# Clustered attention and a SoLU layer on one core: the first token block's turn moves to TensorE, the last block is scaled into w_in's place, and every engine's list is written anew

## The chip, the cores and the metric

The kernel runs on one core of one Trainium2 chip. The metric is the device time of one execution in microseconds (us), lower is better. Times before the change: 224.88 us, the median of three runs (224.47 to 226.29).

## The reference

Two parts follow each other. The first is attention in which a query sees only the keys of its own cluster; the second is a feed-forward layer over the heads' outputs.

```python
B, H, S, D = 4, 8, 768, 64                 # 16 clusters per head
q_assign = argmax(q_n @ c_n.T)             # q_n, k_n, c_n: rows divided by their norm
k_assign = argmax(k_n @ c_n.T)
mask = q_assign[..., :, None] == k_assign[..., None, :]
scores = where(mask, (q @ k.T) / sqrt(D), -1e9)
attn = exp(scores - max(scores)); attn = attn / sum(attn)
x = (attn @ v), as 3072 tokens x 512       # 4 x 768 tokens, 8 heads x 64
h = x @ w_in                               # 512 x 1024
sm = exp(h - max(h)) / sum(exp(h - max(h)))
solu = h * sm
ln = (solu - mean(solu)) / sqrt(var(solu) + 1e-6) * g_ln
out = ln @ w_out                           # 1024 x 512
```

## The kernel before

Everything is written as named operations that are added to a planner (class `Weave`). An operation has an engine, a cost, the operations that it needs, and a function that records its instructions. The order of the operations on each engine is not computed: it is written out by hand as five strings, `ORDER["PE"]` and so on, in which `S3` means the next three operations of kind S. A second table, `AWAY`, names operations that run on another engine than their default (ACT, DVE or POOL; the table "POOL" holds placements that would otherwise be DMAs of SP). The planner's costs do not set the order on an engine; the engines run their lists in order and wait on semaphores.

The names that the text uses, with the lines at which the profile shows them:

- **tp**, **xa**, **xb** (batch 0 only): PE turns 128 tokens of q or k into head-dim-first form (L395, L402), and a copy brings it from PSUM to SBUF (L421, L429). The later batches are turned by DVE, **xt** (L443).
- **ca**: cast of a turned q or k tile into the bf16 tile `qk` (L467 on ACT, L469 and L471 on DVE or POOL).
- **cl, tb, mx, oh, ot, pl, bl**: the clusters. PE's product with the centroids (L483, L488), then four DVE steps that find the best cluster and write it as one-hot (turn back L496, maximum L509, one-hot L514, turn L520), then the placement of the one-hot into `qk` as extra contraction rows (L532, L539) and a blank (L548). The scores then have the cluster match in them, so that exp gives 0 outside of the cluster.
- **S**: scores of one PSUM bank, two 256-column matmuls in most units (L626). **E**: exp of that bank on ACT (L634). **V**: six 65-column matmuls for attn @ v of 128 queries and one head (L653), the 65th column being the sum. **N**: DVE divides by it and writes the bf16 tile `x` (L665, L678). A V of a new group waits for the N of the group before, because there is one `ops` tile. S has three PSUM banks of its own, and the two first banks of `hreg` up to the feed-forward part.
- **cv**: cast of v to bf16 (L557). **su, ce**: g_ln is folded into w_out and its column mean taken off (L597, L606, DVE). **wi**: cast of w_in to bf16 into the tile `w_in_sb` (L577, POOL).
- For each of the 24 blocks f of 128 tokens: **tx** brings x into transposed form `xT` (L708, a DMA transpose issued by SP; block 23 by PE, L717, and a DVE copy, L720). **h**: x @ w_in in four pieces of two 512-column matmuls (L739), which fill two of the three banks of `hreg`. **hm**: the maximum (L745, DVE), **ex**: exp with its sum (L751, ACT), **u**: h times exp (L758, DVE), which frees the banks for later h. **bn, ag, at, al**: variance and the scale alpha (L769, L773 on DVE, L779 to L788 on POOL). **tu**: u transposed (L763 by DMA; blocks 22 and 23 by PE, L727, and a copy, L733 or L735). **y**: the product with w_out in four pieces (L808). **sc**: y times alpha (L826 on ACT, L828 on DVE). **ou**: the output DMA (L837); block 23 is written in two halves of 320 and 192 columns, the second (**oz**) by ACT's DMA queue.
- **wm** and **fl**: PE filler (L855), 25 and 2 matmuls each, that keep PE busy before there is work.

In the code before, `turned(f)` pairs the blocks of the first three batches, so that one DMA transpose of 256 rows brings blocks 0 and 1; `f_scale` puts the first half of block 23 into the tile `y`, which has two buffers, so that it waits for the output DMA of block 21.

Of the kernel before, what the change touches and what calls it, by code (L numbers as in the profile page):

```python
# [22 lines left out]
class Weave:  # L23
# [6 lines left out]
        ld4 si ld3 lv ld lg ld2 lo3 lv ld4 lv ld6 lo ld6 lv li4 tx ld3 tx lv2 ld2 tu ld3 lv ld2 tx  # L30
        tu ou ld6 tu ld5 lv tu ld6 ou ld7 tu ld lv ld4 lv ld3 tx ou lv ld2 tu ld2 ou tx ld4 ou tu
        ld3 tx ou ld4 tu ld7 lv2 ld4 tu lv ld6 ou tu2 pl2 ou tx ld6 tx ou lv tu pl3 tx ou2 tu2 lv tu
        pl tu tx ou tx ou tu tx ou tu tx ou2 tu tx ou tu2 ou tu ou6
    """
    ORDER["POOL"] = """
        pl2 bl pl2 ca bl pl cv pl z ca4 pl2 ca pl2 z bl ca cv2 sg pl4 bl ca pl2 z cv2 pl2 bl ca2 cv2
        ca wi8 ca pl4 ca z cv2 z ca2 at2 bl al ca2 pl3 cv ca pl at ca cv2 pl2 at al pl2 ca al cv2 bl
        at ca2 pl4 al ca bl ca3 pl ca cv pl5 ca al ca2 cv ca2 at2 cv pl2 al ca2 at pl3 ca cv at cv
        al pl bl cv ca3 al at pl2 ca pl2 bl al pl cv pl cv4 at bl ca3 at al2 pl ca al ca2 pl ca pl2
        ca at cv ca3 cv bl pl at pl3 bl al at cv2 po at2 al2 at2 al2 at2 al4 at2 al2 at al  # L40
    """
    ORDER["PE"] = """
        wm fl2 tp2 cp fl2 cl tp2 fl6 cl tp2 S3 cq tp S tp S2 tp2 S3 cl V2 S V S tp S tp S tp gt V3
        S2 tp3 S3 cl S2 V2 S2 V S6 V3 S3 cl S3 V4 S6 V2 S V2 S4 V2 S V2 S2 cl S2 V S V2 S V S2 me2
        S3 V4 S5 cl V S V3 S5 V2 S h4 S2 V2 h2 S3 V3 S V S h S h S2 h V S2 V3 S2 h S V2 S y4 S2 h S
        V S h S2 V3 S2 cl h2 S2 V4 S3 h2 S2 V2 S y2 S2 y S y h V S2 V2 S V S h2 S2 V h V S2 y4 S2 V2
        S cl S3 V4 S2 y S y S2 V2 S V S y S V S V2 S2 y S h S2 V4 S3 cl S V2 S2 cl S3 V2 h S V S V S
        h S2 h V S2 V2 S y S V S y3 V S2 V2 S V S h S h S2 h2 S2 V5 S3 h2 V y2 S3 y2 S2 h S V3 S2 h
        V h S V2 S cl h S3 V2 cl S2 h2 S2 V2 S y S h V2 S3 y3 V2 S h3 S V S2 V2 S V S y2 S2 y2 h V
        S2 V h V S V S2 V2 cl S2 h2 S3 cl S2 V2 S h S V4 S2 y3 S2 y V S2 h S V3 S2 h2 S3 cl V4 S3 y3  # L50
        V2 S y S2 h V2 h S2 h2 S h S h S V2 S y2 S V2 y S3 y V2 S2 h2 S V2 S y S h y3 S V S2 h2 S2 h
        V2 cl S V h2 S y S V S2 V2 S h S V2 S h S2 y V S2 y h2 V2 S2 V2 y S V2 S2 h S h S2 V S V h
        S2 V2 y2 h V S3 h2 S2 V3 S y S y h2 S2 V3 h2 S3 V y4 S h2 S2 V3 S h2 S3 V y2 h2 y2 S3 h2 S2
        V4 y S2 y3 h4 V2 y V2 y3 h ptx h y h2 y3 h2 y4 h2 ptu2 y9 ptu y3 ptu y4
    """
    ORDER["DVE"] = """
        cn xa cb ca2 tb mx oh ot pl2 tb mx xa oh ot xa cf xa3 cv ca tb mx ca oh ot ca gk su xa N xa
        su2 tb mx oh ot N su2 tb mx oh ot N xt N xt su N su xt su N tb xt mx ce N oh ce3 N ce4 hm ot
        N u tb mx N bn hm N bn oh ag ot u xt2 sc hm N bl tb u mx bn2 ca hm N oh ag ot bn u xt2 bn ag
        hm N sc u xt tb mx N oh cv ot bn3 ag xt N sc ca xt2 tb mx N bn oh ot ag tb N mx ca hm ca oh  # L60
# [1256 lines left out]
```

## Time and profile before

| | |
|---|---|
| median of the three runs | 224.88 us |
| the profiled execution, its time | 224.34 us |
| its span, first to last instruction | 222.5 us |
| PE busy | 216.2 us (97%) |
| DVE busy | 201.0 us (90%) |
| ACT busy | 192.9 us (87%) |
| POOL busy | 126.1 us (57%) |

Busy time of PE is the union of its matmuls with their modelled ends, so the time between two starts says more about PE than the busy share. The profile was taken in one execution of 224.34 us, 1.84 us more than the span; the median of the runs lies 0.54 us above that execution.

### The profile page before, as it was taken

How to read it: one execution, taken by the hardware profiler on the slowest of the kernel's cores; microseconds unless marked ns; L12 is line 12 of the kernel's file. 1: busy time of each engine (PE TensorE's matmuls, PEld its weight loads, DVE VectorE, ACT ScalarE, POOL GpSimd, SP SyncE). 2: the span in 40 equal slices, each digit the busy share in tenths (PEclk: the TensorE clock that was granted, in tenths of full speed). 3: DMA queues.
4: the chain of work that ended last, by engine and by line, in shares of the span. 5: the costliest groups of instructions: out<-in, count | busy, mean ns of one | idle time of the engine just before them, and what ended most of it. 6: DMA issues, size and time to landing. Idle time of an engine off the chain costs nothing.

```text
span 222.5 us, 6879 instructions
## 1 busy us (share of the span) xinstructions
PE 216.2 (97%) x2544; PEld 151.3 (68%) x2544; DVE 201.0 (90%) x364; ACT 192.9 (87%) x376; POOL 126.1 (57%) x255
## 2 busy tenths in 40 slices
PE   8999989999999999999999999999999999999993
PEld 7766667667677686877677767677677776665442
DVE  3899989999999999999999998999899698898892
ACT  2899999989999999999988999989899998793351
POOL 3189898937956847668538756628927121024051
PEclk9999999999999999999999999999999999999999
DMA  6999899999998988979998999897961229476533
GB/s 145 363 396 175 176 201 340 202 204 186 206 172 156 199 143 175 206 161 195 189 181 134 239 197 149 120 203 143 222 111 33 52 76 139 115 152 149 153 120 120
DMA packets 123025, 38.92 MB, mean 175 GB/s; under 512 B 111976, under 2 KB 117744, under 8 KB 122992
## 3 DMA queue, kind: packets, MB, share of 16 engines
q1 hardware_dynamic: 122272, 38.00, 82.6%
q10 hardware_dynamic: 720, 0.49, 0.7%
q8 instruction: 20, 0.33, 0.7%
q14 instruction: 13, 0.11, 0.2%
HBM read 23.11 MB, written 6.29 MB: 132 GB/s over the span
## 4 chain that ended last, share of the span: by engine, by line
PE 75%; DVE 16%; DMA 4%; issue 2%; POOL 1%; SPq 1%; DVEq 0%
PE sps L626 22%; PE yps L808 17%; PE hreg L739 17%; PE ops L653 12%; PE csc L488 4%; DVE w_out_c L606 2%; DMA out_dram<-y 2%; PE idle_p L855 2%; DVE w_sum L597 2%; DMA raw<-in_k_dram 2%; DVE oh L514 2%; DVE xt L429 1%; POOL qk L532 1%; DVE xt L443 1%; DVE nmax L745 1%
## 5 line engine op out<-in xcount | busy, mean ns | idle before, releaser
L634 ACT ACTIVATE e<-sps 128x512 bf16<-128x512 f32 (+1 forms) x276 | 143.6, 606 | 8.9 <-PE sps L626 7.4
L626 PE MATMUL sps<-qk 96*128 96x256 bf16 (+5 forms) x600 | 87.8, 263 | 0.1
L626 PEld LDWEIGHTS <-qk 96*128 96x128 bf16 (+1 forms) x636 | 60.0, 121 | 22.8 <-issue 4.6
L653 PEld LDWEIGHTS <-e 128*128 128x128 bf16 x1152 | 48.5, 97 | 10.7 <-DVE x L678 2.5
L653 PE MATMUL ops<-v,e 128*128 128x65 bf16 x1152 | 53.0, 193 | 1.3 <-DVE x L678 1.2
L739 PE MATMUL hreg<-w_in_sb,xT 128*128 128x512 bf16 x192 | 52.0, 379 | 0.2 <-DVE u L758 0.2
L808 PE MATMUL yps<-w_out_c,uT 128*128 128x512 bf16 x184 | 47.1, 379 | 0.0
L539 POOL COPY qk<-oht 32x384 f32<-32x384 f32 (+1 forms) x48 | 23.7, 493 | 36.0 <-DVE oht L520 28.2
L751 ACT ACTIVATE e_sb<-hreg,nmax 128x1024 bf16<-128x1024 f32 x24 | 26.8, 1117 | 7.3 <-DVE nmax L745 7.1
L758 DVE TENSOR_TENSOR u<-e_sb,hreg 128x1024 bf16<-128x1024 bf16 (+1 forms) x25 | 29.1, 1163 | 3.2 <-ACT e_sb L751 3.0
L769 DVE BATCH_NORM_STATS2 bs<-u 128x6 f32<-128x512 bf16 x48 | 31.2, 678 | 0.2
L745 DVE TENSOR_REDUCE nmax<-hreg 128x1 f32<-128x1024 f32 x24 | 29.1, 1211 | 2.1 <-PE hreg L739 1.8
L808 PEld LDWEIGHTS <-uT 128*128 128x128 bf16 x200 | 18.6, 98 | 13.1 <-issue 0.3
L739 PEld LDWEIGHTS <-xT 128*128 128x128 bf16 x192 | 17.3, 97 | 12.7 <-issue 1.2
L785 POOL TENSOR_SCALAR esq<-es,mv 128x1 f32<-128x1 f32 x24 | 8.5, 355 | 30.5 <-DVE mv L773 23.7
L443 DVE STREAM_TRANSPOSE xt<-raw 128x768 f32<-128x768 f32 x24 | 22.4, 953 | 0.0
L471 POOL TENSOR_SCALAR qk<-xt 64x768 bf16<-64x768 f32 x25 | 21.1, 844 | 1.7
L469 POOL CAST qk<-xt 64x768 bf16<-64x768 f32 (+1 forms) x25 | 20.4, 818 | 1.0
L678 DVE TENSOR_TENSOR x<-ops,den 128x256 bf16<-128x256 f32 (+1 forms) x39 | 18.9, 486 | 1.3
L557 POOL CAST v<-vf 128x384 bf16<-128x384 f32 x29 | 14.7, 526 | 1.4 <-DMA vf<-in_v_dram 0.8
L788 POOL TENSOR_TENSOR alpha<-esq,halves 128x1 f32<-128x1 f32 x24 | 13.4, 560 | 2.0
L779 POOL TENSOR_SCALAR es<-esum 128x1 f32<-128x1 f32 x24 | 5.1, 219 | 13.1 <-ACT e_sb L751 12.6
(85 smaller groups left out, 202.2 us busy)
## 6 DMA issues: line engine op xcount, KB each, us to landing
vf<-in_v_dram SPq DMA_DIRECT2D x16, 384.0 KB, 4.4
out_dram<-y SPq DMA_DIRECT2D x23, 256.0 KB, 2.4
raw<-in_q_dram SPq DMA_DIRECT2D x50, 96.0 KB, 3.5
raw<-in_k_dram SPq DMA_DIRECT2D x50, 96.0 KB, 3.2
w_g<-in_moe_w_out_dram SPq DMA_DIRECT2D x4, 512.0 KB, 7.4
w_st<-in_moe_w_in_dram SPq DMA_DIRECT2D x4, 512.0 KB, 7.0
raw<-in_q_dram SPq DMA_DIRECT2D x3, 384.0 KB, 6.4
raw<-in_k_dram SPq DMA_DIRECT2D x3, 384.0 KB, 7.2
```

The source lines that it names most:

```text
L443: nc.vector.transpose(xt[:], raws[b, p, i][:].rearrange("p j c -> p (j c)"))
L471: VEC[e].tensor_scalar(dst, src, scalar1=inv_C, scalar2=1.0, op0=Alu.mult, op1=Alu.mult)
L539: ins = VEC[e].tensor_copy(dst.bitcast(F32), src.bitcast(F32).unsqueeze(1) .to_broadcast([NB, 2, n // 2]))
L626: ins = nc.tensor.matmul(sps_[n, k][:, c0:c0 + w], side(b, h // 2, 1, h % 2, keys)[r], side(b, h // 2, 0, h % 2, slice(s0 * P, s0 * P + w) ...
L634: ins = nc.scalar.activation(es[n, k][:, :w], sps_[n, k][:, :w], Act.Exp, scale=exp_scale, bias=-exp_scale)
L653: nc.tensor.matmul(opss[g][:, s, :VW], es[n, k][:, c0:c0 + P], v1[slot(b, h // 2)][:, h % 2, kt, :VW], start=(kt == 0), stop=(kt == n_t - 1))
L739: uses(nc.tensor.matmul(hreg[:, at(f, f2)[1], :], xTs[f][:, dc, :], w_in_sb[:, dc, f2 * FF2:(f2 + 1) * FF2], start=(dc == 0), stop=(dc == ...
L745: uses(nc.vector.tensor_reduce(ff[f, "nmax"][:], pair_of(f), axis=AXY, op=Alu.max, negate=True), *both(f))
L751: uses(nc.scalar.activation(ff[f, "e"][:], pair_of(f), Act.Exp, bias=ff[f, "nmax"][:], accum_out=ff[f, "esum"][:]), *both(f))
L758: uses(nc.vector.tensor_tensor(ff[f, "u"][:, r], ff[f, "e"][:, r], pair_of(f)[:, r], op=Alu.mult), *both(f)[r])
L769: nc.vector.bn_stats(ff[f, "bs"][:, f2, :], ff[f, "u"][:, f2, :])
L808: ins = nc.tensor.matmul(dst, ff[f, "uT"][:, at(f, f2)[0] * (n_fc // 2) + c, :], w_out_c[:, fc, cols], start=(fc == fcs[0] and turn == 0 i ...
```

## The change

The kernel does the same arithmetic. Block 0's x is turned by PE into the PSUM tile that the clusters use (pool `ps_m`, tag "m"), as an operation `ptx0` of four 128x128 transposes, and copied by DVE (`tx0`); block 1 gets a DMA transpose of its own of 128 rows (`tx1`). The two halves of the last block are scaled into `w_in_sb`, whose contents are not needed any more, instead of a `y` and an `e_sb` buffer, and the first half no longer needs `ou21`. All five lists and the table `AWAY` are new. The lists' text is not shown; it is a table.

```diff
     def turned(f):
-        return list(range(f - f % 2, f - f % 2 + 2)) if f < (B - 1) * n_t else [f]
+        return list(range(f - f % 2, f - f % 2 + 2)) if 2 <= f < (B - 1) * n_t else [f]
...
     def turn_x_pe(f):
         b, su = divmod(f, n_t)
         take_x(f)
-        ff[f, "xp"] = ps_s.tile([P, n_dc, P], BF16, name="xtp", tag="sps")
+        pool, tag = (ps_m, "m") if f == 0 else (ps_s, "sps")
+        ff[f, "xp"] = pool.tile([P, n_dc, P], BF16, name="xtp", tag=tag)
...
     def f_scale(f, e, half=None):
-        if half:
-            y = mo.tile([P, n_ff2, FF2], BF16, name="e_sb")[:].rearrange(
-                "p a f -> p (a f)").bitcast(F32)
+        if half is not None:
+            y = w_in_sb[:, half, :].bitcast(F32)
...
+            if f == 0:
+                add("ptx0", "PE", 0.24, s, lambda e: turn_x_pe(0), nd, take="m")
+                add("tx0", "DVE", 0.36, s, lambda e: keep_x(0, e), ["ptx0"], give="m",
+                    also={"ACT": 0.5})
...
             add(f"sc{f}.0", "DVE", 0.46, s + 5, (lambda e, f=f: f_scale(f, e, 0)),
-                [f"y{f}.2", f"al{f}", f"ou{f - 2}"], also={"ACT": 0.52})
+                [f"y{f}.2", f"al{f}"], also={"ACT": 0.52})
...
     ORDER["ACT"] = """
-        wa xb xa ca xa2 xb ca2 xa E9 ca2 E3 xa3 E3 xa E3 ca E53 ex E11 ...
+        wa xa2 ca2 xa2 xb ca4 E6 xa E2 xa E xa ca E3 xa3 E4 ca E2 xa E53 ex E13 ...
```

In the changed file the line numbers are one higher up to the token functions, and four or five higher in the feed-forward part. Three places of the new order matter below.

The first is the start of ACT's list, from the warm-up to the first exp (L634, L635). `xt_235` and `xt_233` are the turned k of the first pair of heads, `xt_229` and `xt_227` its q, `qk0` the cast tile; `xt_328` and `xt_351` belong to the next pair. Before:

```order
L861 ACTIVATE warm_138<-halves_135 128x1
L421 COPY xt_235<-ops_217 128x3x64
L421 COPY xt_235<-hreg_111 128x3x64
L467 ACTIVATE qk0_99<-xt_235 64x384
L421 COPY xt_229<-hreg_111 128x2x3x64
L421 COPY xt_235<-hreg_111 128x3x64
L421 COPY xt_235<-ops_273 128x3x64
L467 ACTIVATE qk0_99<-xt_235 64x384 x2
L429 COPY xt_328<-hreg_111 128x384
L634 ACTIVATE e_340<-sps_332 128x384
```

And in the change:

```order
L865 ACTIVATE warm_138<-halves_135 128x1
L422 COPY xt_227<-hreg_111 128x2x3x64
L422 COPY xt_233<-hreg_111 128x3x64
L468 ACTIVATE qk0_99<-xt_227 64x384 x2
L422 COPY xt_227<-hreg_111 128x2x3x64
L422 COPY xt_233<-hreg_111 128x3x64
L422 COPY xt_233<-ops_274 128x3x64
L468 ACTIVATE qk0_99<-xt_227 64x384
L468 ACTIVATE qk0_99<-xt_233 64x384 x3
L635 ACTIVATE e_338<-sps_326 128x384
```

ACT now casts both heads' q first, and between the last copy (from `ops`) and the first exp stand four casts of 384 columns, where there were two and a copy.

The second place is DVE's list in the middle of batch 0: from the maximum of the fourth pair's clusters (L509, L510), over the divisions of groups 2 and 3 (RECIPROCAL and TENSOR_TENSOR), to the turn of batch 1's first k (the second L443, L444). Before:

```order
L509 TENSOR_REDUCE mx_721<-cst_702 128x24
L514 TENSOR_TENSOR oh_748<-cst_702,mx_721 128x384
L520 STREAM_TRANSPOSE oht_760<-oh_748 128x384
L665 RECIPROCAL den_770<-ops_712 128x4
L678 TENSOR_TENSOR x_538<-ops_712,den_770 128x2x2x64
L443 STREAM_TRANSPOSE xt_779<-raw_387 128x768
L665 RECIPROCAL den_821<-ops_783 128x4
L678 TENSOR_TENSOR x_538<-ops_783,den_821 128x2x2x64
L443 STREAM_TRANSPOSE xt_836<-raw_529 128x768
```

And in the change:

```order
L510 TENSOR_REDUCE mx_733<-cst_708 128x24
L666 RECIPROCAL den_749<-ops_710 128x4
L679 TENSOR_TENSOR x_557<-ops_710,den_749 128x2x2x64
L515 TENSOR_TENSOR oh_760<-cst_708,mx_733 128x384
L598 SCALAR_TENSOR_TENSOR w_sum_118<-w_g_114,g_ln2_115,w_sum_118 128x512
L521 STREAM_TRANSPOSE oht_809<-oh_760 128x384
L666 RECIPROCAL den_820<-ops_769 128x4
L679 TENSOR_TENSOR x_557<-ops_769,den_820 128x2x2x64
L444 STREAM_TRANSPOSE xt_830<-raw_364 128x768
L444 STREAM_TRANSPOSE xt_853<-raw_552 128x768
```

The division of group 2 now stands ahead of the one-hot and its turn, and both turns of batch 1's first tiles stand behind the division of group 3.

The third place is DVE's list around the maximum of block 18 and its u (TENSOR_REDUCE and L758, L763), with the output scale of block 14 (L828, L832). Before:

```order
L745 TENSOR_REDUCE nmax_4316<-hreg_111 128x1
L665 RECIPROCAL den_4329<-ops_4257 128x4
L678 TENSOR_TENSOR x_3642<-ops_4257,den_4329 128x256
L828 TENSOR_SCALAR y_4344<-yps_4318,alpha_4229 128x512
L758 TENSOR_TENSOR u_4354<-e_sb_4333,hreg_111 128x1024
L769 BN_STATS bs_4396<-u_4354 128x6 x2
```

And in the change:

```order
L750 TENSOR_REDUCE nmax_4280<-hreg_111 128x1
L666 RECIPROCAL den_4318<-ops_4289 128x4
L679 TENSOR_TENSOR x_3624<-ops_4289,den_4318 128x256
L774 BN_STATS bs_4268<-u_4144 128x6
L778 BN_AGGR mv_4344<-bs_4062 128x2
L763 TENSOR_TENSOR u_4348<-e_sb_4322,hreg_111 128x1024
L774 BN_STATS bs_4376<-u_4235 128x6
L832 TENSOR_SCALAR y_4387<-yps_4194,alpha_4354 128x512
```

The scale of block 14 now stands behind block 18's u, not ahead of it.

More of the change, by code (lines that the diff above doesn't have):

```diff
@@ L34 @@
+        tu ld9 ou tu ld4 lv2 ld4 pl tu ou tx ld3 tu tx ld4 ou tu2 ou lv tx lv ou pl3 tu3 ou tx2 ou2
+        tu tx tu tx tu ou2 tx ou tu2 ou tu ou6
     """
     ORDER["POOL"] = """
[L36 to L39, printed above, removed]
@@ L48 @@
[L48 to L52, printed above, removed]
@@ L71 @@
+        tu sc2 oz
     """
@@ L717, in turn_x_pe, with keep_x @@
             nc.tensor.transpose(ff[f, "xp"][:, dc, :], x[:, dc * P:(dc + 1) * P], ident_b[:])
-    def keep_x(f):
-        nc.vector.tensor_copy(xTs[f], ff[f, "xp"][:])
+    def keep_x(f, e="DVE"):
+        if e == "ACT":
+            nc.scalar.copy(xTs[f], ff[f, "xp"][:])
+        else:
+            nc.vector.tensor_copy(xTs[f], ff[f, "xp"][:])
     def turn_u_pe(f, f2):
```

79 lines of the change are left out of this document (43 added, 36 removed).

## The prediction, as put on record

> **What bounds the kernel now.** I read the page first (PE 97% busy, DVE 90%, ACT 87%), then busy time by stretches, then the waits and the timeline of PE, ACT and DVE where PE's starts have holes. The stretches split the kernel in three (a row is the stretch and its length, then the busy time of PE, PE's weight loads, DVE, ACT and POOL with their instructions, the granted clock, the DMA share and GB/s):
>
> ```profile
> 10.00:46.00 36.00, 34.72 (x453) 24.24 (x452) 34.67 (x67) 35.51 (x77) 29.63 (x51) 1.00 0.97 251
> 46.00:200.00 154.00, 153.68 (x1802) 109.70 (x1800) 144.12 (x246) 144.64 (x276) 86.55 (x167) 1.00 0.87 159
> 200.00:222.50 22.50, 18.74 (x130) 9.77 (x127) 16.50 (x30) 7.96 (x14) 6.86 (x17) 0.98 0.48 136
> ```
>
> From 46 to 200 us PE is full: a new order can win almost nothing there, and what it loses there is lost. From 10 to 46 us three engines are full at once, ACT first (35.51 of 36.00), then PE and DVE; a delay on ACT or DVE there comes out as a wait of PE. PE's waits that last over 0.2 us between its starts are few:
>
> ```profile
> 29.00 0.38 PE L626 MATMUL hreg<-qk 96*128 96x256 bf16 x2
> 30.33 0.55 PE L653 MATMUL ops<-v,e 128*128 128x65 bf16 x12 [0.95 <-DVE x L678]
> 30.72 0.38 PE L626 MATMUL hreg<-qk 96*128 96x256 bf16 x2
> 30.94 0.54 PE L653 MATMUL ops<-v,e 128*128 128x65 bf16 x12
> 31.32 0.82 PE L626 MATMUL sps<-qk 96*128 96x256 bf16 x6
> ...
> 42.60 0.60 PE L626 MATMUL sps<-qk 80*128 80x256 bf16 x4
> 43.41 0.55 PE L653 MATMUL ops<-v,e 128*128 128x65 bf16 x12 [0.21 <-DVE x L678]
> 44.05 1.89 PE L739 MATMUL hreg<-w_in_sb,xT 128*128 128x512 bf16 x8
> ```
>
> A bank of scores holds PE 0.22 us (30.72 to 30.94), a V 0.19 us (two from 30.94 to 31.32). So the hole at 30.33 is 30.33 - 29.00 - 0.22 = 1.1 us, and that at 43.41 is 43.41 - 42.60 - 0.44 = 0.4 us. Both wait for DVE's division. Together with two of 0.2 us near 48 us, one of 0.4 at 189 and one of 0.2 at 207 they make 2.5 us: all that an order can still take from PE behind the first scores.
>
> **The change, part by part.**
>
> *Block 0's turn.* PE gets four transposes, DVE a copy; SP's transfer shrinks from 256 to 128 rows and only block 1 waits for it.
>
> ```profile
> 204.03 0.22 PE xtp L717 x4
> ...
> 205.57 0.41 DVE L720 COPY xT<-xtp 128x512 bf16<-128x512 bf16 x1
> ...
> 40.11 1.33 SPq L708 DMA_TRANSPOSE xT<-x  x1
> ...
> xT<-x SPq DMA_TRANSPOSE x14, 3.7
> ```
>
> The same four transposes of block 23 hold PE 0.22 us, the copy holds DVE 0.41. The transfer left at 40.11 and with the usual 3.7 us to landing it came at about 43.8, just ahead of the first h at 44.05: it was hidden, and taking it away wins at most 0.2 us. The four transposes stand among V and S at about 41 us, ahead of PE's wait at 43.41, so they are absorbed as long as PE waits for DVE there (0 here, 0.22 if not). The PSUM tile is that of the clusters, so batch 1's second cluster product is queued behind `tx0` on DVE. On PE-mode transposes the Trainium skill (TensorE: Matmul & The Clock Gate, Part 4) gives about 275 ns for one of 128x128 in a kernel and says that they do not keep the clock up. By that page this edit would cost 1.1 us and the sum below would be 0.9 us higher; the trace has 0.22 us for all four, at a granted clock of 0.98 over the last stretch.
>
> *ACT's start.* Here I see the first loss.
>
> ```profile
> 7.63 0.70 ACT L421 COPY xt<-hreg 128x384 f32<-128x384 f32 x2 [0.73 <-PE hreg L395]
> 8.59 1.06 ACT L467 ACTIVATE qk<-xt 64x384 bf16<-64x384 f32 x2
> 9.67 0.51 ACT L429 COPY xt<-hreg 128x384 f32<-128x384 f32 x1
> 10.16 3.74 ACT L634 ACTIVATE e<-sps 128x384 bf16<-128x384 f32 x9
> ...
> 12.87 1.50 PE L483 MATMUL csc<-xt,w_out_c 128*32 128x384 f32 x16
> ...
> 14.43 0.58 DVE L496 STREAM_TRANSPOSE cst<-csc 128x384 f32<-128x384 f32 x1
> ```
>
> The copies from 7.63 to 8.59 wait for PE in either order. Behind them stand four casts of 0.53 us (1.06 for two) in place of two and a copy: the first exp starts at 8.59 + 2.12 = 10.7, not 10.16. Then come six exps of 0.37 (ten starts from 10.16 to 13.9) and, new on ACT, the copy of the second pair's last k, 0.5: done at 10.7 + 2.2 + 0.5 = 13.4. The cluster product L483 needs that copy; it started at 12.87 and now starts at 13.45, so DVE's turn back moves from 14.43 to 15.0: **+0.57**.
>
> *DVE up to the first feed-forward block.* Between that turn back and the division that ends PE's wait at 43.41, DVE's list has the same work but for a cast of v and `tx0` more (a cast and a copy swap with like ones):
>
> ```profile
> 13.66 0.39 DVE L557 CAST v<-vf 128x384 bf16<-128x384 f32 x1
> ...
> 31.52 0.18 DVE L665 RECIPROCAL den<-ops 128x4 f32<-128x4 f32 x1 [0.36 <-PE ops L653]
> ...
> 43.27 2.71 DVE L606 SCALAR_TENSOR_TENSOR w_out_c<-w_g,g_ln,hreg 128x512 bf16<-128x512 f32 x4
> 46.04 1.22 DVE L745 TENSOR_REDUCE nmax<-hreg 128x1 f32<-128x1024 f32 x1
> ```
>
> 0.39 + 0.41, less some 0.1 each by which neighbours overlap, is **+0.6**. DVE's one idle stretch there, 0.36, is filled in the new order, since both turns of batch 1 now follow the division: **-0.36**. DVE is then 0.57 + 0.6 - 0.36 = 0.8 later at 43, and still at 46.04, where the first maximum started right behind `w_out_c` (43.27 + 2.71 = 45.98). Moving group 2's division ahead of the one-hot does shorten PE's wait at 30.33, by about the two steps passed (0.56 and 0.58), but DVE is the same length to 43, so what PE wins at 30 it waits later, first at batch 1's cluster product, which needs the turns that have moved back. From 46 on PE follows the maximum by way of exp and the next banks. I take **+0.8** for PE at 50 us; bounds -0.6 (the 0.57 does not arise, DVE has nothing more to do and PE keeps some of the 1.1) and +1.5 (the wait for the turns on top).
>
> *Block 18.* The scale that stood ahead of u waited for an output DMA:
>
> ```profile
> 188.01 0.75 DVE L828 TENSOR_SCALAR y<-yps,alpha 128x512 f32<-128x512 f32 x1 [1.01 <-DMA out_dram<-y]
> 188.68 1.21 DVE L758 TENSOR_TENSOR u<-e_sb,hreg 128x1024 bf16<-128x1024 bf16 x1
> ...
> 189.31 0.40 PE L626 MATMUL sps<-qk 80*128 80x128 bf16 x4
> 189.94 1.04 PE L739 MATMUL hreg<-w_in_sb,xT 128*128 128x512 bf16 x4 [0.23 <-DVE u L758]
> ```
>
> PE waited 189.94 - 189.31 - 0.22 = 0.4 for that u. The scale now stands behind u, so the wait can go, though h also comes 0.7 sooner behind the block before: **-0.3** (-0.4 to 0). What is late next is the maximum of block 19, if the DMA is still out.
>
> *ACT in the full stretch.* Seven scales come to ACT, three scales and two copies of u leave it.
>
> ```profile
> L826 ACT ACTIVATE y<-yps,alpha 128x512 f32<-128x512 f32 x12 | 8.3, 694 | 3.2 <-PE yps L808 2.2 <-DVE mv L773 0.7 <-POOL alpha L788 0.3
> L735 ACT COPY uT<-utp 128x512 bf16<-128x512 bf16 x3 | 1.6, 584 | 0.0
> ```
>
> 4 x 0.69 less 2 x 0.58 is 1.6 us more; ACT has 154.00 - 144.64 = 9.4 us idle from 46 to 200, which hides most. In the worst place (block 10) a wide exp of 1.1 (the row at 207.37 below) and a scale of 0.7 stand one bank apart, while three banks of scores cover about as much: **+0.3** (0 to 0.6).
>
> *The end.*
>
> ```profile
> 218.65 0.55 DVE L828 TENSOR_SCALAR y<-hreg,alpha 128x320 f32<-128x320 f32 x1 [1.15 <-PE hreg L808]
> 219.11 0.41 DVE L828 TENSOR_SCALAR e_sb<-hreg,alpha 128x192 f32<-128x192 f32 x1
> 219.55 0.35 ACTq L837 DMA_DIRECT2D out_dram<-e_sb  x1
> ```
>
> Two scales ran one after the other on DVE; now the 320-column half is on ACT. The last DMA leaves when both are done, about 0.2 earlier: **-0.2** (-0.4 to 0). The wait for block 21's output was not the last to end (218.65 follows PE's last products), so dropping it wins nothing by itself.
>
> The sum is 0.8 - 0.3 + 0.3 - 0.2 = +0.6 us, on the profiled execution 224.34 + 0.6 = 224.9. The median of the runs is 0.54 above that execution; the forecast for a median is 224.88 + 0.6 = **225.5 us**.
>
> **The rivals.**
>
> *The start costs nothing* (ACT's casts run while PE and DVE are behind anyway): without the +0.57, and with ACT's +0.3 hidden, the sum is -0.3: 224.6. For it: DVE's list to 43 us is no longer in total, because casts moved off it at the start. Against it: DVE idles at 14.4 then, and from 8 to 46 us ACT has no gap to give back.
>
> *Faster: all of PE's holes close.* The 2.5 us, and 0.2 at the end, less 0.2 for the transposes: 222.4. For it: the two largest holes are divisions, and the new list puts one of them two steps earlier. Against it: from 10 to 46 us DVE and ACT are full, so a hole closed moves on.
>
> *Slower: the loops of blocks 16 to 22.* Each block runs last h, maximum, exp, u, and only then the next block's last h may overwrite the bank.
>
> ```profile
> 184.60 0.84 PE L626 MATMUL sps<-qk 80*128 80x128 bf16 x12
> 185.24 1.21 DVE L745 TENSOR_REDUCE nmax<-hreg 128x1 f32<-128x1024 f32 x1
> ...
> 206.05 1.23 DVE L745 TENSOR_REDUCE nmax<-hreg 128x1 f32<-128x1024 f32 x1
> 207.37 1.11 ACT L751 ACTIVATE e_sb<-hreg,nmax 128x1024 bf16<-128x1024 f32 x1 [3.00 <-DVE nmax L745]
> 208.61 1.22 DVE L758 TENSOR_TENSOR u<-e_sb,hreg 128x1024 bf16<-128x1024 bf16 x1 [0.45 <-ACT e_sb L751]
> 209.94 1.03 PE L739 MATMUL hreg<-w_in_sb,xT 128*128 128x512 bf16 x4
> ```
>
> That takes 209.94 - 206.05, about 4.0 us with the handoff. Counted with the holds above (h and y 0.43 each), the new order leaves PE 4.31, 4.05, 4.24, 4.24, 4.28, 4.22 and 3.88 us of other work; before it was 4.47, 4.21, 4.91, 4.12, 4.24, 4.00 and 3.88. Where a statistic of 0.6 stands ahead of the maximum, as at 185.24 (0.64 behind the last h, which ended when PE went on at 184.60), a loop is 4.6. From a mean delay of 0.2 on, every loop makes PE wait; at 0.6 the seven lose about 0.4 each: 225.5 + 2.8 = 228.3. Against it: most of these loops kept their time before with as little slack.
>
> **How the numbers follow.** The forecast's own case 0.48, its neighbour without the start's loss 0.20, all holes closed 0.10, the loops (or a like loss in the full stretch) 0.22. A measurement of this kernel can tell about 1% from no change, 2.2 us: below 222.6 faster, above 227.1 slower. So faster 0.10, same 0.68, slower 0.22. The range of 223.6 to 228.0 takes in the start at either bound and the loops at most of their price; it leaves out the case of all holes closed and the far end of the slow one.
>
> **What would show it.** Right: the first exp at 10.7, the cluster product at 13.4 or later, the first wide maximum near 46.8, no wait for an output DMA ahead of block 18's u, and the two last scales side by side. Wrong: the maximum at 46.0 or sooner (the start's loss is not there), PE under 153 us busy of the same 154 (the loops or ACT), or a start-to-start of `ptx0`'s four transposes far over 0.22.

## The result, and the profile after

The change takes 223.93 us (median of 15 runs, 223.39 to 224.49) against 224.97 us before (15 runs, 223.89 to 226.29): a ratio of 0.996, interval 0.9942 to 0.9977. It is 1.0 us faster; the forecast was 225.5, 0.6 slower. Ratios leave out runs more than 1.5% above the fastest of their kernel, so a ratio can be nearer to 1 than the medians are (e7 below).

The profiled executions do not show that 1.0 us: 224.34 before, 224.38 after. The one of before lies 0.63 below its median, the one of after 0.45 above. The stretches of the profile after (columns as in the prediction):

```profile
10.00:46.00 36.00, 34.82 (x453) 24.60 (x454) 33.79 (x67) 35.48 (x79) 28.16 (x50) 1.00 0.91 244
46.00:200.00 154.00, 152.12 (x1776) 109.65 (x1802) 144.58 (x248) 144.84 (x279) 88.51 (x166) 1.00 0.84 160
200.00:222.50 22.50, 18.88 (x132) 10.11 (x132) 16.13 (x30) 9.09 (x15) 6.99 (x18) 0.99 0.46 132
```

ACT has no more slack than before, and DVE is 0.9 us lighter up to 46. PE's 152.12 is no loss: 30 matmul records of h and y are missing in this trace (177 and 185 of them where the weight loads are 192 and 200). So PE is read from its starts. Timeline of ACT, PE and DVE at the places of the prediction:

```profile
8.68 2.02 ACT L468 ACTIVATE qk<-xt 64x384 bf16<-64x384 f32 x4
10.61 2.34 ACT L635 ACTIVATE e<-sps 128x384 bf16<-128x384 f32 x6
13.61 0.85 PE L484 MATMUL csc<-xt,w_out_c 128*32 128x384 f32 x8
30.24 0.54 PE L654 MATMUL ops<-v,e 128*128 128x65 bf16 x12
47.13 1.23 DVE L750 TENSOR_REDUCE nmax<-hreg 128x1 f32<-128x1024 f32 x1
188.26 1.22 DVE L763 TENSOR_TENSOR u<-e_sb,hreg 128x1024 bf16<-128x1024 bf16 x1
190.00 0.73 DVE L832 TENSOR_SCALAR y<-yps,alpha 128x512 f32<-128x512 f32 x1
218.79 0.53 ACT L830 ACTIVATE w_in_sb<-hreg,alpha 128x320 f32<-128x320 f32 x1 [0.87 <-PE hreg L813]
219.13 0.42 DVE L832 TENSOR_SCALAR w_in_sb<-hreg,alpha 128x192 f32<-128x192 f32 x1 [1.40 <-PE hreg L813]
```

The first exp is at 10.61 (forecast 10.7), the cluster product at 13.61 (13.4 or later), the first wide maximum at 47.13 (46.8). The V at 30.24 no longer waits. Block 18's u has no wait for a DMA ahead of it, PE's four transposes of block 0 hold it 0.22 us (41.11 to 41.33), and the two last scales run side by side. The marks named in advance came as told, and yet the sum is wrong. Four marks that every trace has cut an execution into pieces that add up to its span: the first V of group 3 (30.33 before, 30.24 after), the first wide maximum, the start of PE's last matmul (218.54 and 218.77), the end.

| us | to that V | V to maximum | maximum to last matmul | last matmul to end | span |
|---|---|---|---|---|---|
| before | 30.33 | 15.71 | 172.49 | 3.93 | 222.46 |
| after | 30.24 | 16.89 | 171.64 | 3.60 | 222.38 |

The new head (all up to 51 us) is 1.1 later at the maximum, the body behind it gives 0.85 back and the end 0.33.

### The profile page after: what moved, and what is told of

Its sections match the earlier page's. It is cut to its first block, busy times and chain, and to the rows that moved or that the text cites. A ratio compares the mean times of both kernels' runs of the same rounds, so it can differ in the third digit from the quotient of the medians.

```text
span 222.4 us, 6852 instructions
## 1 busy us (share of the span) xinstructions
PE 214.8 (97%) x2518; PEld 151.8 (68%) x2548; DVE 199.1 (90%) x363; ACT 194.7 (88%) x382; POOL 126.6 (57%) x252
## 4 chain that ended last, share of the span: by engine, by line
PE 91%; DVE 3%; issue 2%; ACT 2%; DVEq 0%; ACTq 0%
PE sps L627 27%; PE hreg L744 18%; PE yps L813 17%; PE ops L654 16%; PE csc L489 4%; PE hreg L627 2%; PE idle_p L859 2%; PE csc L484 1%; PE hreg L403 1%; PE hreg L396 1%; ACT qk L468 1%; PE hreg L813 1%; ACT e L635 1%; DVE u L763 1%; DVE w_sum L598 1%
## 5 line engine op out<-in xcount | busy, mean ns | idle before, releaser
L635 ACT ACTIVATE e<-sps 128x512 bf16<-128x512 f32 (+1 forms) x276 | 143.2, 609 | 10.2 <-PE sps L627 9.8
L654 PEld LDWEIGHTS <-e 128*128 128x128 bf16 x1152 | 49.9, 97 | 9.3 <-issue 1.9
L654 PE MATMUL ops<-v,e 128*128 128x65 bf16 x1152 | 54.3, 193 | 0.4 <-DVE x L679 0.4
L744 PE MATMUL hreg<-w_in_sb,xT 128*128 128x512 bf16 x177 | 48.3, 378 | 0.8
L813 PE MATMUL yps<-w_out_c,uT 128*128 128x512 bf16 x169 | 45.1, 379 | 0.8
L540 POOL COPY qk<-oht 32x384 f32<-32x384 f32 (+1 forms) x49 | 24.2, 494 | 21.5 <-DVE oht L521 15.7
L763 DVE TENSOR_TENSOR u<-e_sb,hreg 128x1024 bf16<-128x1024 bf16 (+1 forms) x25 | 29.1, 1169 | 2.7 <-ACT e_sb L756 2.1
L813 PEld LDWEIGHTS <-uT 128*128 128x128 bf16 x200 | 18.0, 97 | 13.1 <-issue 0.3
L472 POOL TENSOR_SCALAR qk<-xt 64x768 bf16<-64x768 f32 (+1 forms) x27 | 22.2, 823 | 3.5 <-DVE xt L444 1.7
L444 DVE STREAM_TRANSPOSE xt<-raw 128x768 f32<-128x768 f32 x24 | 22.2, 949 | 0.0
L470 POOL CAST qk<-xt 64x768 bf16<-64x768 f32 (+1 forms) x25 | 20.9, 836 | 1.2
L784 POOL TENSOR_SCALAR es<-esum 128x1 f32<-128x1 f32 x24 | 5.6, 236 | 20.9 <-ACT e_sb L756 20.4
L830 ACT ACTIVATE y<-yps,alpha 128x512 f32<-128x512 f32 x15 | 10.4, 695 | 4.3 <-PE yps L813 3.0
```

Of the source, the lines that this page charges most:

```text
L444: nc.vector.transpose(xt[:], raws[b, p, i][:].rearrange("p j c -> p (j c)"))
L472: VEC[e].tensor_scalar(dst, src, scalar1=inv_C, scalar2=1.0, op0=Alu.mult, op1=Alu.mult)
L540: ins = VEC[e].tensor_copy(dst.bitcast(F32), src.bitcast(F32).unsqueeze(1) .to_broadcast([NB, 2, n // 2]))
L635: ins = nc.scalar.activation(es[n, k][:, :w], sps_[n, k][:, :w], Act.Exp, scale=exp_scale, bias=-exp_scale)
L654: nc.tensor.matmul(opss[g][:, s, :VW], es[n, k][:, c0:c0 + P], v1[slot(b, h // 2)][:, h % 2, kt, :VW], start=(kt == 0), stop=(kt == n_t - 1))
L744: uses(nc.tensor.matmul(hreg[:, at(f, f2)[1], :], xTs[f][:, dc, :], w_in_sb[:, dc, f2 * FF2:(f2 + 1) * FF2], start=(dc == 0), stop=(dc == ...
```

## The experiments

My theories were four. A: the two edits carry the gain. B (later E): the order behind 51 us, the "body", carries it. D, then H: in the old "head" loads land when they are needed, and executions in which they are late make the median. F: the 1.1 us hole at 30 us tips PE's clock. Each batch had 35 runs of before on its own chip (medians 224.57, 224.49, 224.78, 224.61); every other kernel had 12 runs.

**Edits, head and body.** The lists were cut at 51 us, where both hold the same steps; names are as in the planner.

```diff
 e1_edits: lists of before
+SP: tx1 in tx0's place    DVE: oh1.0 tx0 ce1
-PE: S16.0 S16.1 cl1.1 V14.0 S16.2 V14.1 V15.0 V15.1
+PE: S16.0 S16.1 ptx0 V14.0 S16.2 V14.1 V15.0 cl1.1 V15.1
+ACT: sc22 sc23.0 oz23     (both halves into w_in_sb)
 e2_order: lists of the change
-PE: ptx0    DVE: tx0    ACT: sc23.0
+SP: tx0 (blocks 0 and 1)    DVE: tu23.1 sc23.0 sc23.1    (into y and e_sb)
 e3_head: new lists to 51 us, those of before behind; both edits
 e4_body: lists of before to 51 us, new ones behind; both edits
```

> The lists of before with the two edits alone: block 0's x turned by PE (ptx0 behind S16.1, tx0 behind the one-hot of batch 1's first clusters, batch 1's second cluster product moved back behind V15.0), and the last halves scaled into w_in's place, the first of them on ACT. The two profiles are alike in time (224.34 and 224.38) though the medians differ by 1.0 us, so part of the gain lies in what varies between executions. Theory A, the edits carry it (the end 0.3 shorter, and the 256-row transfer that landed at 43.9, 0.15 us ahead of the first h, is no longer late in some executions): 1.0 below before, and the runs lie as close together as those of the change (1.1 us from lowest to highest, against 2.4 of before). Theory B, the order behind 50 us carries it: 0.1 to 0.3 below before, from the end alone, and the spread of before stays. Theory C, all three add up to nothing that one part explains: between the two.

> The new lists without the two edits: blocks 0 and 1 again turned by one DMA transpose of 256 rows, no ptx0 and no tx0 on DVE, the last halves scaled as before (DVE, one behind the other, into y and e_sb, behind block 21's output DMA). Theory A (edits): no more than 0.2 from before. Theory B (order behind 50 us): 0.7 below before. My prediction's working, ACT's start 0.57 late and DVE 0.4 later at 43 us: 0.5 to 0.8 above before.

> The new lists up to about 51 us (up to u of block 0 on DVE and the bank of scores ahead of h1.1.0 on PE) with both edits, the lists of before from there on. Theory A: 1.0 below before, as the change. Theory B: 0.3 to 0.8 above before, since the new head puts PE 0.8 to 1.1 us later at 50 us and the old body gives none of it back, less 0.3 at the end. If the body takes a late head back by itself (PE waits less later, because other engines get ahead): within 0.3 of before.

> The lists of before up to about 51 us with both edits, the new lists from there on: the reverse of the head alone. Theory A: 1.0 below before, as the change. Theory B: 1.5 to 2.0 below before, because the head of before is 0.8 to 1.1 us ahead at 50 us and the new body keeps that lead, so this version would beat the change. If a lead at 50 us is not kept: equal to the change, 1.0 below before.

| | median (range) | ratio to before, interval |
|---|---|---|
| e1_edits | 225.23 (224.07 to 227.38) | 1.0027, 0.9986 to 1.0067 |
| e2_order | 224.25 (223.83 to 225.79) | 0.9973, 0.9943 to 1.0004 |
| e3_head | 224.48 (224.18 to 224.98) | 0.9979, 0.9953 to 1.0006 |
| e4_body | 223.81 (222.90 to 224.99) | 0.9962, 0.9935 to 0.9990 |

A fell: the edits alone win nothing. With the new body the time is that of the change, whichever head. The new head wins less by itself (the intervals overlap), but its runs lie within 0.8 us. In the trace of e4, with the old head, PE waits for POOL's cast of v, and that for its load (waits, 26 to 50 us: total, times, longest):

```profile
POOL v L560 <- DMA vf<-in_v_dram: 3.9, 1, 3.9
PE ops L656 <- POOL v L560: 1.7, 1, 1.7
```

**Is it that load?** The same load (lv0.3, v of batch 0's fourth pair) moved both ways.

```diff
 SP of before (e5, and e8 = e4 with the same move; e7 below)
 ld1.0.1
+lv0.3
 ld1.1.0.0 ld1.1.0.1 lo3 ld1.1.0.2 ld1.1.0 ld1.1.1.0 ld1.1.1.1 ld1.1.1.2 ld1.1.1
-lv0.3
 li0 li1 li2 li3
 e7: lv0.3 behind li1          e6: lists of the change, lv0.3 behind ld1.1.1
```

> Before with one load moved in SP's list: lv0.3, the v of batch 0's fourth pair (128x2x1536 bytes, 384 KB), stands behind ld1.0.1 as in the change, nine loads sooner than in before, where it is the last one ahead of the four of w_in. In the traces of before, of the edits alone and of the old head with the new body this load landed at 36.3, 37.9 and 38.5 us, its cast on POOL (cv0.3.0) ended 0.5 later and the first V of the fourth pair (V12.0) began at 38.2, 38.6 and 39.2, with a wait of PE of 0, 0.73 and 1.88 us ahead of it; with the lists of the change it landed at 31.5 and nothing waited. Theory D, this load is what the gain comes from: landing near 32 us, no wait ahead of V12.0, median 0.5 to 1.0 below before, and the runs within 1.2 us of each other where those of before span 2.4 to 4.2. Theory E, the order behind 50 us carries the gain and the load only the upper tail: the median within 0.3 of before, the upper tail gone. Against both: moving it holds back the k of batch 1 by 1 us each, and DVE's turns wait instead: equal to before or slower.

> The change with the same load moved back, behind ld1.1.1 and ahead of w_in as in before. Theory D: landing near 37 to 39 us, PE waits up to 2 us ahead of V12.0 in part of the executions, the median 0.5 to 1.0 above the change (equal to before) and the runs spread over 2 us or more. Since the new head is about 0.8 us later at that place, it hides that much of the lateness: at least 0.3 above. Theory E: the median 0.8 to 1.0 below before as the change has it.

> Before with that load two places later still, behind the second of the four loads of w_in: a larger dose. Those two loads landed 1.3 and 2.2 us apart, so it lands 2.5 to 3.5 us later, at 39 to 41 us, in every execution. Theory D: PE waits 2 to 3 us ahead of V12.0, and the median is 1.0 to 2.5 above before (part of the wait is given back at V16.0, where PE waited 0.4 for a division, and the casts of w_in come sooner). Theory E: 0 to 1.0 above. The granted clock: in the longest executions of before and of the edits (227 us and more) it stood at 0.991 to 0.992, else at 0.996 to 1.0. If a wait of PE of 2 to 3 us takes the clock with it, it is 0.992 or lower in most runs here; if the clock has nothing to do with it, it stays at 0.996 to 1.0.

> The lists of before up to 51 us with both edits, the new ones behind it (224.41 in the profile, median 223.81), with that load behind ld1.0.1. Theory D: its 1.88 us wait ahead of V12.0 is gone, the median 0.5 to 1.0 lower than without the move: 222.8 to 223.3, below the change, and the spread 1.2 us or less. Theory E: within 0.3 of the version without the move. If PE's lead at 50 us is lost again behind it, because other engines bound there: 223.8, as the change.

| | median (range) | ratio to before, interval |
|---|---|---|
| e5, before, early | 225.35 (223.88 to 226.87) | 1.0012, 0.9974 to 1.0049 |
| e6, change, late | 223.82 (223.42 to 224.35) | 0.9958, 0.9934 to 0.9983 |
| e7, before, later still | 228.16 (224.77 to 230.87) | 1.0070, 1.0023 to 1.0117 |
| e8, e4 with it early | 223.41 (223.17 to 225.17) | 0.9955, 0.9928 to 0.9982 |

D fell as a theory of this one load: early it wins nothing in before, late it costs the change nothing; in e8 the median is 0.4 lower than in e4, the ratio only 0.0007, within the intervals. But the dose of e7 shows what a late load does in the old head, and e5 and e7 show PE's clock. Timeline of PE in e7, then its clock in e5 (stretch, five busy times, then the clock):

```profile
37.97 0.38 PE L630 MATMUL sps<-qk 80*128 80x256 bf16 x2
42.08 1.48 PE L657 MATMUL ops<-v,e 128*128 128x65 bf16 x24 [3.73 <-POOL v L561]
```

```profile
28.00:30.00 2.00, 1.35 (x11) 0.80 (x9) 1.83 (x4) 2.00 (x5) 1.87 (x4) 1.00 0.99 170
30.00:31.00 1.00, 0.25 (x8) 0.26 (x9) 0.97 (x4) 0.84 (x2) 0.90 (x3) 1.00 0.75 238
31.00:32.00 1.00, 1.00 (x26) 0.91 (x23) 0.58 (x1) 0.73 (x2) 0.88 (x4) 0.83 1.05 308
32.00:33.00 1.00, 1.00 (x6) 0.73 (x5) 0.94 (x3) 0.85 (x2) 0.94 (x3) 0.50 1.36 188
33.00:34.00 1.00, 1.00 (x13) 0.80 (x11) 1.00 (x2) 1.00 (x4) 0.89 (x4) 0.50 0.74 104
34.00:35.00 1.00, 1.00 (x17) 0.87 (x15) 0.18 (x1) 0.70 (x3) 0.94 (x2) 0.50 1.04 166
35.00:36.00 1.00, 1.00 (x16) 0.62 (x18) 0.59 (x3) 0.82 (x2) 1.00 (x2) 0.97 1.46 147
```

In e5 PE is idle 0.65 of 28 to 30 us and 0.75 of the next; from 31.7 to 35.1 its clock is 0.50. In e7 it is 0.50 for twice as long, from 40.3 to 47.1 us: it falls about 2 us into the wait shown. In e8 another load is late instead: the last k of batch 1's second pair lands at 38.4, its turn on DVE begins 0.1 later, and PE waits 1.1 us at `ptx0` for the division behind that turn.

**Which list?** One step, then SP's list alone in both directions, then the old start.

```diff
 e9, DVE of before
 tb0.3 mx0.3
+N2
 oh0.3 ot0.3
-N2
 e10: before, SP's list to 51 us as in the change
 e11: the change, SP's list to 51 us as in before
 e12: the change, first 15 us of PE, ACT, DVE, POOL as in before
```

> Before with one step moved on DVE: the division of group 2 (N2) stands ahead of the fourth pair's one-hot and its turn, as in the change. In five traces of the old head PE waits 1.08 to 1.11 us for it ahead of V6.0 at 28.1 to 29.4 us. Two of the traces (before with the load early, and with it later still) show PE at half its clock for about 3.4 us, from 31.8 and from 42.1 us, each time behind such waits (0.6 and 1.1 us following each other; 3.9 us), with a mean granted clock of 0.990 and 0.985. Theory F, the hole at V6.0 is what tips the clock and costs the median as well: the hole shrinks to 0.3 or less, no run of 12 has a clock of 0.992 or lower (before: 5 of 70), and the median is 0.5 to 1.0 below before. Theory H, late loads are what varies, and the order behind 50 us the rest: clock drops become rarer, but the median stays within 0.4 of before, because DVE is the same length to 43 us and PE waits later.

> Before with SP's list of the change up to 51 us (which load is issued when), all other lists as before, neither edit. In the change's four traces the loads of the first 40 us land 3 to 5 us ahead of their use (v of the fourth pair 4.2 to 4.4, k of batch 1's second pair 3.0 to 3.6), in those of the old head 0 to 2 us ahead. Theory H with the loads as the cause: the spread falls to that of the change (1.1 us) and the median is 0.4 to 0.8 below before, 0.3 to 0.6 above the change. If the slack comes from the other lists, which use the same tiles later: no change in the median against before, runs up to 226 remain.

> The change with the SP list of before up to 51 us, the reverse of the one above. Theory H with the loads as the cause: 0.4 to 0.8 above the change, with single runs at 226. If the slack comes from the lists of DVE, POOL and PE (the moved load alone cost the change nothing): within 0.3 of the change, the runs within 1.3 us.

> The change with the first 15 us of PE, ACT, DVE and POOL as before (ACT's two casts and a copy ahead of the first exp in place of four casts), SP's list and all that follows as in the change. In the traces PE has waited 1.4 to 1.5 us in all by 10 us with the new start, 0.2 to 1.1 with the old one, and the first cluster product of the second pair stood at 13.6 against 12.9. If the start's loss is real and lasts (term of +0.57 of the prediction): 0.4 to 0.7 below the change, 223.2 to 223.5, a version better than both. If the engines that bind behind it make it up: within 0.2 of the change. If the new start is what gives the later loads their slack: 0.3 or more above it, with a wider spread.

| | median (range) | ratio to before, interval |
|---|---|---|
| e9, N2 ahead | 225.15 (224.51 to 226.14) | 1.0016, 0.9987 to 1.0044 |
| e10, before, new loads | 224.63 (223.81 to 229.45) | 0.9990, 0.9964 to 1.0017 |
| e11, change, old loads | 223.96 (223.42 to 227.47) | 0.9970, 0.9947 to 0.9992 |
| e12, change, old start | 223.61 (223.15 to 224.49) | 0.9941, 0.9917 to 0.9965 |

No run of e9 has a mean clock of 0.992 or lower, but its median is not below that of before, so F does not explain the median. In e9 the hole at 30 us is closed, and PE waits at the next V and the next scores for POOL (timeline of PE):

```profile
29.21 0.54 PE L657 MATMUL ops<-v,e 128*128 128x65 bf16 x12
32.53 0.54 PE L657 MATMUL ops<-v,e 128*128 128x65 bf16 x12 [0.79 <-POOL v L561]
35.76 0.28 PE L630 MATMUL sps<-qk 80*128 80x256 bf16 x1 [0.65 <-POOL qk L475]
```

The test is not clean, though. The last step of su on DVE (`w_sum`), which runs at that time, takes 2.20 us in e9 where it takes 0.70 in before; POOL casts qk and v beside it all that time (timeline of DVE, before and then e9):

```profile
35.77 0.70 DVE L597 SCALAR_TENSOR_TENSOR w_sum<-w_g,g_ln,w_sum 128x512 f32<-128x512 f32 x1
35.82 2.20 DVE L601 SCALAR_TENSOR_TENSOR w_sum<-w_g,g_ln,w_sum 128x512 f32<-128x512 f32 x1
```

That is more than the 1.1 us of the hole, so e9 does not tell what the hole alone costs.

SP's list is not what makes the change's runs alike (e11 without its one run at 227.47 spans 0.9 us). e12 has the lowest ratio of all versions, though its interval overlaps that of the change: the start costs 0.35 us by the medians of this batch (e11 and e12), 0.4 by the ratios of the change and e12. In the traces the stretch from the first exp to the V of group 3 is 19.22 us in e12 and 19.63 with the new start (after, e6, e11); one DVE step in it (`w_sum` again) takes 0.75 and 1.2 us.

**The terms on an even head.** With e12 as the base, one thing put back at a time (in another batch than e12; the median of before was 224.78 there and 224.61 here).

```diff
 e13: e12, lists of before behind 51 us (both edits kept)
 e14: e12, DVE
-ag14 u18 bn17.0 sc14
+ag14 sc14 u18 bn17.0
 e15: e12, ACT: -sc23.0   DVE: +sc23.0 ahead of sc23.1, into y and e_sb, behind ou21
 e16: e12, PE: -ptx0   DVE: -tx0   SP: tx0 for both blocks in tx1's place
```

> The version with the old start (e12, 0.994 of before) with the lists of before from 51 us on; both edits stay. Trace of before against those of the change from 50 us to PE's last matmul: PE waits 3.4 against 2.5 to 3.05, and the last y to the end is 0.1 longer with the old list. Theory H, the body is worth 0.4 to 0.9 whatever the head: 0.4 to 0.9 above e12, 0.996 to 0.998 of before. If it was the old head's late loads alone that the new body swallowed: within 0.2 of e12.

> The version with the old start (e12) with one step put back: block 14's scale on DVE stands ahead of block 18's u again. The prediction gave that step 0.3 (0 to 0.4). If it holds: 0.3 above e12 and in the trace a wait of PE of 0.2 to 0.4 ahead of h19.1.0, behind a DVE wait for the output DMA of block 12. If the scale fits there because this head and body leave the DMA more time: within 0.15 of e12 and no such wait.

> The version with the old start (e12) with the old end: both halves of block 23 scaled on DVE, one behind the other, into y and e_sb, the first one behind block 21's output DMA. From the start of PE's last matmul to the end the traces show 3.92 to 3.94 us with the old list and end, 3.81 with the new list and the old end, 3.60 with both new. So 0.21 above e12, with 3.81 in the trace; the prediction gave this edit 0.2 (0 to 0.4).

> The version with the old start (e12) without PE's four transposes and DVE's copy: blocks 0 and 1 turned by one DMA transpose of 256 rows again. PE's four transposes stand in its list with no wait around them to absorb them, so leaving them out saves 0.22 on PE, and 0.41 on DVE ahead of w_out's last columns: 0.2 to 0.5 below e12 if the transfer lands ahead of the first h (at 43.7 to 44.1 in three traces, against a first h at 44.1 to 45.1). If it lands later than that in most executions: 0 to 0.4 above e12, with a wait of PE ahead of h0.0.0. The prediction said 0, absorbed.

| | median (range) | ratio to before, interval | median against e12 | in the trace, against e12 |
|---|---|---|---|---|
| e13, old body | 224.12 (223.66 to 225.93) | 0.9975, 0.9945 to 1.0006 | +0.5 | maximum to last matmul 172.09, not 171.63; end +0.10 |
| e14, scale ahead | 224.80 (224.28 to 225.15) | 0.9984, 0.9957 to 1.0010 | +1.2 | maximum to last matmul 173.20 |
| e15, old end | 223.79 (223.47 to 224.05) | 0.9949, 0.9925 to 0.9974 | +0.2 | end 3.81, not 3.60 |
| e16, DMA turn | 223.96 (223.39 to 225.25) | 0.9961, 0.9934 to 0.9989 | +0.35 | V to maximum 17.24, not 16.89 |

All four intervals overlap that of e12 (0.9917 to 0.9965), so the sizes rest on the traces.

The wait of e14 is not the one I expected (DVE's scale, then PE's h):

```profile
188.02 0.75 DVE L834 TENSOR_SCALAR y<-yps,alpha 128x512 f32<-128x512 f32 x1 [1.13 <-POOL alpha L795]
189.96 0.82 PE L746 MATMUL hreg<-w_in_sb,xT 128*128 128x512 bf16 x3 [1.40 <-DVE u L765]
```

In the new list the last step of block 14's variance stands just ahead of u, so a scale there waits for POOL's alpha, not for an output DMA. In e16 the 256-row transfer landed at 44.5 us and the first h began at 44.64, 0.35 after PE was ready. In e2, with the later start of the change, the same transfer landed at 44.1, a full 1.0 ahead of the first h, and cost nothing (V to maximum 16.89).

**Before, profiled again.**

```diff
 e17, e18: before, unchanged
```

> The kernel before, unchanged: a second profiled execution. Theory H (before's own executions differ up to the first wide maximum, by loads that land as late as they are used): if this one takes over 225, the stretch from V6.0 to the first maximum is 16.3 us or more against 15.71 in the first look, with a wait ahead of V12.0, V14.0 or h0.0.0 behind a load, and from 50 us to the end PE waits 3.3 to 3.5 as in the first look. Rival: the stretch is 15.5 to 15.8 again and the difference lies at the start (first exp 9.3 to 10.6) or behind 50 us.

> The kernel before, unchanged: a third profiled execution. The same as for the second look: over 225 us goes with a longer stretch from V6.0 to the first maximum (theory H), or with the start or the stretch behind 50 us (rival). If it takes 224.5 or less, theory H wants 15.5 to 16.0 there.

They took 224.00 and 224.53, so neither is one of the executions of over 225 us, of which before had 52 in the 140 runs of the four batches. Nine traces with one set of marks (us); "full clock" is the time from which the trace has PE's granted clock at 1.0:

| | time | full clock | first exp | that V | maximum | V to maximum | maximum to last matmul | end |
|---|---|---|---|---|---|---|---|---|
| before | 224.34 | 6.5 | 10.16 | 30.33 | 46.04 | 15.71 | 172.49 | 3.93 |
| e17 | 224.00 | 4.8 | 9.93 | 30.07 | 45.86 | 15.79 | 172.20 | 3.94 |
| e18 | 224.53 | 4.2 | 9.69 | 29.84 | 46.21 | 16.37 | 172.29 | 3.95 |
| e1_edits | 224.36 | 4.1 | 9.81 | 29.95 | 46.54 | 16.58 | 172.11 | 3.71 |
| e4_body | 224.41 | 3.6 | 9.29 | 29.43 | 47.17 | 17.74 | 171.84 | 3.61 |
| after | 224.38 | 6.9 | 10.61 | 30.24 | 47.13 | 16.89 | 171.64 | 3.60 |
| e6, load late | 223.42 | 3.7 | 9.65 | 29.29 | 46.18 | 16.89 | 171.64 | 3.60 |
| e11, old loads | 223.42 | 4.4 | 9.72 | 29.35 | 46.24 | 16.89 | 171.64 | 3.63 |
| e12, old start | 223.61 | 6.1 | 10.16 | 29.38 | 46.27 | 16.89 | 171.63 | 3.60 |

With the new head the stretch from V to maximum is the same to 0.01 us: 16.89 in nine traces (after, e2, e3, e6, e11 to e15), while the load of the fourth pair's v landed anywhere from 31.0 to 36.3 us in them. What still varies is the first exp, and that goes through to the end. It follows PE's clock, not the loads: the full clock came at 3.7, 4.4, 6.5, 6.8 and 6.9 us in e6, e11, e3, e2 and the change, and the first exp at 9.65, 9.72, 10.48, 10.57 and 10.61; the eighth load of q and k landed sooner in the change (6.2 us) than in e6 (6.7). The same eight filler matmuls take 1.06 us in the change and 0.61 in e6 (timeline of PE, the change and then e6):

```profile
5.72 1.06 PE L859 MATMUL idle_p<-w_out_c 128*128 128x128 bf16 x8
5.13 0.61 PE L863 MATMUL idle_p<-w_out_c 128*128 128x128 bf16 x8
```

With the old lists an earlier V wins nothing: it is 0.5 earlier in e18 than in the first trace of before, and the maximum is 0.2 later. No load was late there; v's landed at 34.7 us, in the other two behind 36. DVE lost the lead in one step, the `w_sum` that took 0.70 us in the first trace:

```profile
35.27 1.31 DVE L597 SCALAR_TENSOR_TENSOR w_sum<-w_g,g_ln,w_sum 128x512 f32<-128x512 f32 x1
```

Here too POOL cast v and qk beside it; in the first trace it was still waiting for v. The rows behind two lines of the table (PE's V and DVE's maximum of e6, then of e18):

```profile
29.29 0.54 PE L658 MATMUL ops<-v,e 128*128 128x65 bf16 x12
46.18 1.23 DVE L754 TENSOR_REDUCE nmax<-hreg 128x1 f32<-128x1024 f32 x1
```

```profile
29.84 0.55 PE L653 MATMUL ops<-v,e 128*128 128x65 bf16 x12 [0.94 <-DVE x L678]
46.21 1.23 DVE L745 TENSOR_REDUCE nmax<-hreg 128x1 f32<-128x1024 f32 x1
```

What stays open: which wait makes before's executions of over 225 us, none of which has a trace. Late loads are shown in variants of before only (e1, e4, e7), so theory H is not shown for before itself; the halved clock can be in the 9 of its 140 runs with a mean clock of 0.992 or lower, and the long `w_sum` is a third candidate that no run tested. Which of the new head's many steps frees it was not found; a single load and SP's list do not, and the division ahead of the one-hot does not in the old list.

## Why the prediction was wrong

The forecast of 225.5 misses by 1.6 us. Two steps failed.

**The median set 0.54 above the profiled execution** ("the forecast for a median is 224.88 + 0.6"): 1.0 of the 1.6. I carried before's distance from profile to median over to the changed kernel, as if it were a constant of the chip. The change's distance is -0.45: its profiled execution was one in which PE's full clock came late (6.9 us; first exp at 10.61, against 9.65 and 9.72 in e6 and e11, whose engine lists are the same), and in this order that goes through to the end. Before's profile had a late clock as well, but the shortest stretch from V to maximum of its three traces. The three times shown already spread over 1.8 us (224.47 to 226.29), and I took nothing of that as a term.

**The body put at nothing** (block 18 -0.3, ACT +0.3): the rest, since the sum of +0.6 came out as +0.04 between the two profiled executions. (There is luck in that split: e6 and e11, with the engine lists of the change and an early clock, took 223.42, 0.9 below the profile of before.) From the first maximum to the last matmul the pair of profiles has -0.85; the other two traces of before make it -0.56 and -0.65. The reading that failed is "all that an order can still take from PE": it counted waits of 0.2 us and more, and before has four of 0.08 to 0.13 us, at 69, 170, 174 and 175 us, three of them for an exp of ACT and one for DVE's division. They are 0.38 us in all, and 0.40 in the other two traces of before. With PE's wait of 0.39 for block 18's u they make 0.77 of the 0.85, and the change has none of the five. The term of block 18 had the right sign, but its wait was only 0.07 and 0.17 us in the other two traces of before. The term of ACT had the wrong sign: behind 51 us the change takes PE's waits for ACT away and adds none. With a new head ahead of it the old body costs 0.27 us (e3 against the change) and 0.46 (e13 against e12) in the traces.

The other steps, each by its own number:
- *ACT's start, +0.57*: the first exp and the cluster product came where told, in part by luck, since PE's full clock came late in both profiles (6.5 and 6.9 us). With an early one the first exp is no later than in before (9.65 and 9.72 in e6 and e11, 9.93 and 9.69 in e17 and e18). As a price of the new lists it is about 0.35 (e12).
- *DVE to 43 us, together +0.8*: +1.09 at the maximum in the pair, of which the late start is a part. Over the traces with whole new head and start (after, e2, e3, e6, e11: maximum at 46.18 to 47.13, mean 46.7) against the three traces of before (46.0) it is +0.7: the term holds against executions of before that took 224.0 to 224.5.
- *The division ahead of the one-hot moves the wait on*: right in the old list (e9); the next wait is for POOL, not for DVE's turns, and a longer DVE step adds to it.
- *Block 0's turn, 0, at most 0.2 to win*: it depends on the head. Put back on the DMA it costs 0.35 in the trace with the old start (e16) and nothing with the start of the change (e2). PE's hold of 0.22 came as told. (Where the prediction sets 1.1 us in place of 0.22, its sum would be 0.7 higher, not 0.9, since the 0.4 of waiting there takes in the rest.)
- *The end, -0.2*: the edit is worth 0.21 (e15), and 0.1 more comes with the new order of the last steps.
- *The start costs nothing* (224.6) came nearest by its number, by luck: the start does cost something (e12). *All holes close* (222.4) came true of the five in the body; in the head the hole at 30.33 closed as well, but others took its place and the maximum came no sooner.
- *The loops of blocks 16 to 22* did not become the bound.

## What to carry to other kernels

One profiled execution tells the path of that execution. Before a sum is made on it, take the spread of the runs as a term of its own: here executions of the same engine lists lay 1.0 us apart by when PE's full clock came. An order in which the delays of loads and engines are taken in (16.89 us from V to maximum in nine traces) can win on the median what no row of a good execution shows; that this is how the change is rid of the long executions of before is likely, but not shown. Add up the waits of 0.1 us as well: here four of them weighed as much as the largest one of the body. A transfer that lands 0.1 us ahead of its use in one execution is not hidden in all (e16). And where a new order is cut in two (head and body, at a place where both lists hold the same steps), the halves can be run crosswise, which tells in four runs in which half the gain lies.

## What the runs showed of the hardware

**PE's clock halved behind waits shorter than a window.** In e5 the granted clock was 0.50 for 3.4 us behind 1.4 us of idle PE within 3 us. In e7 it was 0.50 for 6.8 us, from about 2 us into one wait of 3.7 us. One stretch of 3.4 us costs 3.4 x 0.5 = 1.7 us if PE is busy, and 1.7 of 226 is a mean clock of 0.992: all 18 runs of 227 us and more are at 0.992 or lower. So low a mean came in 9 of 140 runs of before, in 3 of 12 each of e1 and e5, in 8 of 12 with the long wait of e7, and in 1 of 99 with the new lists of the engines from 15 us on. The Trainium skill (TensorE: Matmul & The Clock Gate, Part 1) has the half rate follow one idle window of about 3.4 us that runs freely, and its section on HAM oscillation gives as the rule no idle gap over about 3.4 us. The length of the slow stretch agrees with e5 and e7 (one and two windows); the threshold does not, since the longest gap between PE's starts in e5 was 1.1 us beyond what its matmuls hold. The same gap stood in the three traces of before without a drop.

**The full clock at the start comes at another time in each execution.** In the 20 traces it was granted from 3.6 to 6.9 us on. With the same engine lists the first exp began between 9.65 and 10.61 us, in the order of that time.

**A load scatters.** A load of 384 KB at one place of SP's list (before, e17, e18, e1, e4) was issued at 31.1 to 32.5 us and landed between 34.7 and 38.5 us.

**A DVE step was longer beside POOL's casts.** The last `w_sum` step of 128x512 took 0.70 us in five traces of the old head in which POOL cast next to nothing beside it (before, e17, e1, e4, e7), 0.85 and 0.86 beside a cast of v (e8, e10), 1.31 (e18) and 2.20 (e9) beside casts of v and qk. That the casts are the cause was not tested.
